# Joining the small TensorE steps of a pack attention that runs between the matmuls of an MLP

## The chip, the cores and the metric

The kernel runs on one core of a Trainium2 chip. The metric is the device time in microseconds (us) of one execution. The engines named here are TensorE (PE; PEld is its weight load), VectorE (DVE), ScalarE (ACT), GpSimd (POOL) and SyncE (SP), whose queue issues most DMAs.

## What is computed

A pack attention over 8 batches and 8 heads, with 576 rows and 64 columns per head and 32 packed rows, then two MLPs over its 4608 x 512 output. The reference, cut:

```python
def _attn_ref(q, k, v, p):
    scale = 1.0 / np.sqrt(q.shape[-1])
    def sm_attn(qq, kk, vv):
        s = scale * np.matmul(qq, kk.transpose(0, 1, 3, 2))
        s = s - np.max(s, axis=-1, keepdims=True)
        a = np.exp(s)
        a = a / (np.sum(a, axis=-1, keepdims=True) + 1e-09)
        return np.matmul(a, vv)
    p_packed = sm_attn(p, k, v)
    return sm_attn(q, p_packed, p_packed)

# x: 4608 x 512, w_in: 512 x 2048, w_out: 2048 x 512
h = x @ w_in;   x = (h * (1.0 / (1.0 + np.exp(-h)))) @ w_out          # first MLP
h = x @ w_in2;  out = (h * np.clip(h + 3.0, 0.0, 6.0) / 6.0) @ w_out2  # second MLP
```

## The kernel before

**Blocks.** The first MLP goes through nine blocks `j` of 512 token columns: one for the first 512 rows of each batch (blocks 0 to 7) and one for the 64 remaining rows, the tails, of all batches (block 8). In `block`, 16 slices `f` each have a hidden product (`hidden`, matmuls L874 to L876, one PSUM bank), a SiLU on ScalarE (L882), a split into a rounded part `gh` on ScalarE and a residue `gl` on VectorE (`split_g`, L889 and L890), and, two slices later, a projection (`project`, L897 to L899) into four accumulator banks. Each such matmul has 512 columns. Blocks 0 and 8 have twelve matmuls in a hidden product, blocks 1 to 7 six, since there the packed values have been multiplied into the first weights beforehand (`fuse_steps`, L657 to L659, the "fused" products). After block 8 the second MLP runs by itself.

**Attention between the matmuls.** A group `n` is four heads of a batch, two groups per batch, 16 in all. Groups 0 and 1 are done in an opening written out by hand. Groups 2 to 15 are done in small steps that are put between the big matmuls of blocks 0 to 6. Per group there are: the transposes of packed queries and of key and query tails (`step_kpq`), scores of packed queries against keys (`step_s`, L439) and against key tails (`step_st`, L449), a softmax (`exp1`, `post1`), transposes of its result (`step_t`, L471) and of its tail (`step_tt`, L479), the packed values (`step_pp`, L490 and L493), their transpose (`step_pt`, L513), scores of queries against packed values (called value scores here, `step_z`, L529, and `step_zt`, L538), a second softmax (`exp2`, `post2`), transposes on VectorE (`step_u`, `step_ut`) and the tail output (`step_xt`, L596). Keys and queries of groups from 4 on are transposed on VectorE (`step_tr`, L426). The products of scores and value scores use 64 columns of the array for each half of the heads, and each float32 product is two passes, so a step of this kind has four matmul records.

**PSUM.** Every small step takes a bank by `bank()`. Outside the opening this is the ring of four banks that the hidden products use as well. Four other banks are the accumulators.

**The order.** `WINDOWS` lists for each block which group `c` has its scores and which group `d` its value scores in a window; `b` and `a` are the `c` and `d` of the window before, whose softmaxes come in between. `window` turns that into steps with a cost, what they need and how long they wait behind it. A `Plan` counts ticks, one for each big matmul, and runs a step at a tick when its place in the block has come, its needs are met for so many ticks, and its bank is taken to be free. `hidden` offers a tick behind each half of a hidden product (in blocks 1 to 7), `block` one behind each quarter of a projection. What is left at a block's end is run there by `plan.finish`, with no big matmuls between.

**Loads.** `use` marks an operand as used; `load_next` then issues the loads of the values, queries and keys three entries further in the order of use, on SP's queue (L356, L366, L373). The same queue issues the weight tiles of the first MLP (`next_out`, L260, and `next_in`, L247).

Of the kernel before, what the change touches and what calls it, by code (L numbers as in the profile page):

```python
# [8 lines left out]
F32 = mybir.dt.float32  # L9
# [9 lines left out]
def tile_pack_attention_two_mlps(ctx: ExitStack, tc, q, k, v, p, w_in1, w_out1, w_in2, w_out2, out):  # L19
# [378 lines left out]
    def step_kpq(c, d):  # L398

        ps = bank()  # L400
        if c is not None:
            nc.tensor.transpose(ps[:, 0:P], pair(st.pop(("pbd", c)), 0), ident)
        for a, what, n in (1, "k", c), (2, "q", d):
# [3 lines left out]
            if n is not None:  # L407
                del nat[what, n]
        if c is not None:
# [12 lines left out]
    def step_tr(n, what, j):  # L422
        m = nat.pop((what, n, j))
        if n >= 4:
            t = half_kb(n, "T", 3)
# [5 lines left out]
        t = half_kb(n, "T", 3)  # L431
        copy(out=t, in_=ps)
        st[what, n, j] = t

    def step_s(n):
        kpq = st["kp", n]
        ps = bank()
        for j in range(2):
            mm(ps[j * 64:(j + 1) * 64, :], lhsT=kpq[:, j * 64:j * 64 + 64], rhs=st.pop(("k", n, j)), start=True, stop=True)  # L439
        d1 = d1s.pop(n) if n in d1s else at.tile([P, S], F32, tag="d1", name="d1")  # L440
        copy(out=d1[:, 0:T], in_=ps)
        st["d1", n] = d1

    def step_st(n):
        kpq, d1 = st.pop(("kp", n)), st["d1", n]
        ps = bank()
        for j in range(2):
            o = P + j * TAIL
            mm(ps[j * 64:(j + 1) * 64, 0:TAIL], lhsT=kpq[:, j * 64:j * 64 + 64], rhs=kpq[:, o:o + TAIL], start=True, stop=True)  # L449
        copy_short(out=d1[:, T:S], in_=ps[:, 0:TAIL])  # L450
        m = at.tile([P, 4], F32, tag="s1m", name="s1m", bufs=2)
        nc.vector.reduce_max(out=m[:, 0:1], in_=d1, axis=AX.X)
        nc.vector.tensor_scalar_mul(out=m[:, 1:2], in0=m[:, 0:1], scalar1=-SCALE)
        st["d1", n] = d1, m
# [11 lines left out]

    def step_t(n):
        d1, _ = st["d1", n]
        ps = bank()
        for i in range(NI):  # L470
            nc.tensor.transpose(ps[:, i * P:(i + 1) * P], d1[:, i * P:(i + 1) * P], ident)  # L471
        a = half_kb(n, "T", 3)
        copy(out=a, in_=ps)
        st["a1", n] = a

    def step_tt(n):
        d1, _ = st.pop(("d1", n))
        ps = bank()
        nc.tensor.transpose(ps[0:TAIL, 0:P], d1[:, T:S], ident)  # L479
        a = at.tile([TAIL, P], F32, tag="a1Tt", name="a1Tt")  # L480
        copy_short(out=a, in_=ps[0:TAIL, 0:P])
        st["a1t", n] = a
# [1390 lines left out]
```

## Time and profile before

| | |
|---|---|
| median of 3 runs | 1543.95 us (1542.73 to 1549.97) |
| the profiled execution | 1546.56 us, span 1544.7 us |
| TensorE matmuls in flight | 1505.0 us, 97% of the span |
| VectorE, ScalarE, GpSimd busy | 67%, 51%, 12% |
| mean granted TensorE clock | 0.994 of full speed |
| blocks 0 to 6 of the first MLP | about 38 to 686 us |
| blocks 7 and 8 | to about 846 us |

Times in the views are us from the first instruction unless marked ns. Matmuls are pipelined: a duration reaches from the start of one to the end of its drain, and the next begins before that, so costs on TensorE are read from start times. In a timeline row the brackets tell how long the engine was idle before the instruction and what ended it. L12 is line 12 of the kernel; `128*64 128x512` is a matmul over 128 rows and 64 columns of the array with 512 moving columns, and abank is a bank from `bank()`.

### The profile page before, as it was taken

How to read it: one execution, taken by the hardware profiler on the slowest of the kernel's cores; microseconds unless marked ns; L12 is line 12 of the kernel's file. 1: busy time of each engine (PE TensorE's matmuls, PEld its weight loads, DVE VectorE, ACT ScalarE, POOL GpSimd, SP SyncE). 2: the span in 40 equal slices, each digit the busy share in tenths (PEclk: the TensorE clock that was granted, in tenths of full speed). 3: DMA queues.
4: the chain of work that ended last, by engine and by line, in shares of the span. 5: the costliest groups of instructions: out<-in, count | busy, mean ns of one | idle time of the engine just before them, and what ended most of it. 6: DMA issues, size and time to landing. Idle time of an engine off the chain costs nothing.

```text
span 1544.7 us, 21698 instructions
## 1 busy us (share of the span) xinstructions
PE 1505.0 (97%) x7550; PEld 1224.5 (79%) x7550; DVE 1036.0 (67%) x1695; ACT 780.1 (51%) x1241; POOL 192.5 (12%) x177
## 2 busy tenths in 40 slices
PE   7999999999999999999999999999999999999998
PEld 4667766777777767778887888888888888999998
DVE  6667455755576556653452678877887778778777
ACT  6776546655565446654453334433443444444442
POOL 2433111111211111113241000000000000000000
PEclk9999999999999999999999999999999999999999
DMA  9999787987679777769697667677767776898887
GB/s 241 290 287 313 249 220 208 264 216 195 179 223 253 204 163 214 252 167 245 187 301 213 191 198 241 197 222 225 238 193 223 227 229 201 279 316 254 272 273 218
DMA packets 434508, 358.51 MB, mean 232 GB/s; under 512 B 191200, under 2 KB 325856, under 8 KB 434400
## 3 DMA queue, kind: packets, MB, share of 16 engines
q1 hardware_dynamic: 423632, 343.79, 75.8%
q10 hardware_dynamic: 10768, 13.34, 2.8%
q8 instruction: 61, 1.00, 0.3%
q14 instruction: 47, 0.39, 0.1%
HBM read 295.17 MB, written 61.87 MB: 231 GB/s over the span
## 4 chain that ended last, share of the span: by engine, by line
PE 84%; ACT 5%; DVE 4%; DMA 3%; SPq 2%; issue 2%; POOL 1%; ACTq 0%; DVEq 0%; POOLq 0%
PE b L1148 7%; PE b L1150 7%; PE b L1149 7%; PE b L1243 7%; PE acc L897 7%; PE b L1245 7%; PE b L1246 7%; PE acc L898 7%; PE acc L899 7%; PE hps L874 4%; PE hps L876 4%; PE hps L875 4%; PE abank L439 1%; PE abank L657 1%; PE abank L529 1%
## 5 line engine op out<-in xcount | busy, mean ns | idle before, releaser
L890 DVE TENSOR_TENSOR gl<-hps,gh 128x512 fp32r<-128x512 f32 x144 | 98.8, 686 | 165.9 <-ACT gh L889 165.5
L1245 PE MATMUL b<-ro,ws 128*128 128x512 f32 (+2 forms) x564 | 206.2, 366 | 0.0
L1246 PE MATMUL b<-ro,ws 128*128 128x512 f32 (+2 forms) x564 | 206.2, 366 | 0.0
L1148 PE MATMUL b<-xc,ws 128*128 128x512 f32 (+1 forms) x560 | 205.6, 367 | 0.0
L1150 PE MATMUL b<-xc,ws 128*128 128x512 f32 (+1 forms) x560 | 205.6, 367 | 0.0
L1149 PE MATMUL b<-xc,ws 128*128 128x512 f32 (+1 forms) x560 | 205.5, 367 | 0.0
L1191 DVE TENSOR_TENSOR ro<-g,ro 128x1024 fp32r<-128x1024 f32 (+1 forms) x140 | 161.4, 1157 | 42.1 <-ACT ro L1186 41.8
L1186 ACT CAST ro<-g 128x1024 fp32r<-128x1024 f32 (+1 forms) x140 | 132.1, 967 | 93.8 <-DVE g L1179 34.5
L882 ACT ACTIVATE hps<-hps 128x512 f32<-128x512 f32 x144 | 84.1, 584 | 113.9 <-PE hps L876 113.2
L1243 PE MATMUL b<-ro,ws 128*128 128x512 f32 (+2 forms) x564 | 139.0, 367 | 0.3
L897 PE MATMUL acc<-gh,wr 128*128 128x512 f32 x288 | 117.5, 408 | 3.2 <-ACT gh L889 3.2
L897 PE MATMUL acc<-gh,wo 128*128 128x512 f32 x288 | 116.8, 406 | 0.0
L1245 PEld LDWEIGHTS b<-ro,ws 128*128 128x128 f32 x564 | 105.9, 188 | 13.1
L1246 PEld LDWEIGHTS b<-ro,ws 128*128 128x128 f32 x564 | 105.9, 188 | 13.1
L1150 PEld LDWEIGHTS b<-xc,ws 128*128 128x128 f32 x560 | 105.1, 188 | 13.2
L1149 PEld LDWEIGHTS b<-xc,ws 128*128 128x128 f32 x560 | 105.1, 188 | 13.2
L1148 PEld LDWEIGHTS b<-xc,ws 128*128 128x128 f32 x560 | 105.1, 188 | 13.1
L1243 PEld LDWEIGHTS b<-ro,ws 128*128 128x128 f32 x564 | 102.9, 188 | 15.1 <-DVE ro L1191 2.2
L898 PE MATMUL acc<-gl,wr 128*128 128x512 f32 x288 | 113.8, 395 | 0.5 <-DVE gl L890 0.5
L899 PE MATMUL acc<-gh,wr 128*128 128x512 f32 x288 | 113.3, 393 | 0.0
L898 PE MATMUL acc<-gl,wo 128*128 128x512 f32 x288 | 112.6, 391 | 0.5 <-DVE gl L890 0.5
L899 PE MATMUL acc<-gh,wo 128*128 128x512 f32 x288 | 112.6, 391 | 0.0
(310 smaller groups left out, 2899.7 us busy)
## 6 DMA issues: line engine op xcount, KB each, us to landing
ws<-w2in SPq DMA_DIRECT2D x280, 256.0 KB, 3.2
ws<-w2out SPq DMA_DIRECT2D x280, 256.0 KB, 3.4
wi<-w1i SPq DMA_DIRECT2D x80, 512.0 KB, 5.5
wo<-w1o SPq DMA_DIRECT2D x64, 512.0 KB, 5.5
x1d<-x SPq DMA_DIRECT2D x18, 512.0 KB, 5.6
w1i<-win SPq DMA_DIRECT2D x16, 512.0 KB, 6.9
praw<-in_moe_w_in_dram SPq DMA_DIRECT2D x32, 256.0 KB, 5.5
praw<-in_moe_w_out_dram SPq DMA_DIRECT2D x32, 256.0 KB, 5.8
```

Source lines behind the costliest of these rows:

```text
L890: nc.vector.tensor_sub(out=gl, in0=g, in1=f32(gh))
L897: mm(acc[e], lhsT=w[:, 0, s], rhs=gh, start=first, stop=False)
L898: mm(acc[e], lhsT=w[:, 0, s], rhs=gl, start=False, stop=False)
L899: mm(acc[e], lhsT=w[:, 1, s], rhs=gh, start=False, stop=last)
L1148: mm(ps, lhsT=wh, rhs=xs[k][:, 0, c], start=first, stop=False, skip_group_check=True)
L1149: mm(ps, lhsT=wh, rhs=xs[k][:, 1, c], start=False, stop=False, skip_group_check=True)
L1150: mm(ps, lhsT=wl, rhs=xs[k][:, 0, c], start=False, stop=last, skip_group_check=True)
L1186: nc.scalar.copy(out=t[:, 0], in_=v)
L1191: nc.vector.tensor_sub(out=t[:, 1], in0=self.operand(s), in1=f32(t[:, 0]))
L1243: mm(to, lhsT=wh, rhs=x, start=False, stop=last, skip_group_check=True)
L1245: mm(to, lhsT=wh, rhs=x, start=first, stop=False, skip_group_check=True)
L1246: mm(to, lhsT=wl, rhs=x, start=False, stop=False, skip_group_check=True)
```

## The change

`step_kpq` now also does the transposes of `step_t` and `step_tt` for the group before, in two banks. `step_zs` replaces `step_z`, `step_zt`, `step_s` and `step_st`: value scores, scores, both tails, and, outside block 0, the transpose of packed values and the tail output of the groups before, in three banks; the engines that read them come behind all products. In block 1 the value scores of groups 4 and 5 move one window back. The planner lets one step take several banks and finish several keys, holds a fourth tile of transposed data (`T`, four buffers for three, in all functions that allocate it), and takes the loads of the next values when the joined step is issued. The packed values of groups 0 and 1 get tiles of their own in place of ones that weight tiles use later. `step_pt` and `step_xt` are cut in two, product and copy. The steps that these replace are taken out; the rest of the diff passes the new arguments on.

```diff
-    def step_kpq(c, d):
-
+    def step_kpq(c, d, b):
+
+        if b is not None:
+            d1, _ = st.pop(("d1", b))
+            rows = bank()
+            for i in range(NI):
+                nc.tensor.transpose(rows[:, i * P:(i + 1) * P], d1[:, i * P:(i + 1) * P], ident)
         ps = bank()
+        if b is not None:
+            nc.tensor.transpose(ps[0:TAIL, 3 * P:], d1[:, T:S], ident)
         if c is not None:
             nc.tensor.transpose(ps[:, 0:P], pair(st.pop(("pbd", c)), 0), ident)
...
+        if b is not None:
+            st["a1", b] = half_kb(b, "T", 4)
+            copy(out=st["a1", b], in_=rows)
+            st["a1t", b] = at.tile([TAIL, P], F32, tag="a1Tt", name="a1Tt")
+            copy_short(out=st["a1t", b], in_=ps[0:TAIL, 3 * P:])
         if c is not None:
             t = at.tile([P, 2 * P], F32, tag="kp", name="kp")
             copy(out=t, in_=ps[:, 0:2 * P])
...
     def value_pp(n, ps):
         r = st.pop(("r1", n))
         if n < QPB:
-            pf, on = half_kb(1, "ppf")[:, 0:HQ * D].rearrange("p (h d) -> p h d", h=HQ), mask
+            pf, on = at.tile([P, HQ, D], F32, tag="ppf0", name="ppf0", bufs=2), mask
         else:
             pf, on = at.tile([P, 2, D], F32, tag="ppf", name="ppf", bufs=3), twos
...
+    def step_pt(n, ps=None):
+        ps = bank() if ps is None else ps
+        nc.tensor.transpose(ps[:, 0:P], pair(st["pp", n], 0), ident)
+        st["ps", "pt", n] = ps
+
+    def step_ptc(n):
         t = at.tile([P, P], F32, tag="ppT", name="ppT", bufs=4)
-        copy_short(out=t, in_=ps[:, 0:P])
+        copy_short(out=t, in_=st.pop(("ps", "pt", n))[:, 0:P])
         st["ppT", n] = t
 
 
...
+    def step_zs(c, d, b, a):
+
+        if d is not None:
+            t, z = st["ppT", d], bank()
+            for j in range(2):
+                o = (1 - j if turned(d // QPB) else j) * 64
+                mm(z[o:o + 64, :], lhsT=t[:, j * 64:j * 64 + 64], rhs=st.pop(("q", d, j)), start=True, stop=True)
+        if c is not None:
+            kpq, ps = st.pop(("kp", c)), bank()
+            for j in range(2):
+                mm(ps[j * 64:(j + 1) * 64, :], lhsT=kpq[:, j * 64:j * 64 + 64], rhs=st.pop(("k", c, j)), start=True, stop=True)
+        rest = bank()
+        if d is not None:
+            qt = st.pop(("qt", d))
+            for j in range(2):
+                mm(rest[j * 64:(j + 1) * 64, TAIL:2 * TAIL], lhsT=t[:, j * 64:j * 64 + 64], rhs=qt[:, j * TAIL:(j + 1) * TAIL], start=True, stop=True)
+        if c is not None:
+            for j in range(2):
+                o = P + j * TAIL
+                mm(rest[j * 64:(j + 1) * 64, 0:TAIL], lhsT=kpq[:, j * 64:j * 64 + 64], rhs=kpq[:, o:o + TAIL], start=True, stop=True)
+        if b is not None:
+            step_pt(b, rest[:, P:2 * P])
+        if a is not None:
+            step_xt(a, rest[:, 2 * P:3 * P])
+        if d is not None:
+            nc.vector.transpose(out=d2s[d][:, 0:T], in_=z)
+        if c is not None:
+            d1 = d1s.pop(c) if c in d1s else at.tile([P, S], F32, tag="d1", name="d1")
+            copy(out=d1[:, 0:T], in_=ps)
+        if d is not None:
+            nc.vector.transpose(out=d2s[d][:, T:S], in_=rest[:, TAIL:2 * TAIL])
+            g = S // NP
+            m = at.tile([P, g, 1], F32, tag="s2m", name="s2m")
+            dv = d2s[d].rearrange("p (g s) -> p g s", s=NP)
+            nc.vector.reduce_max(out=m[:, :, 0], in_=dv, axis=AX.X)
+            nc.vector.tensor_tensor(out=dv, in0=dv, in1=m.to_broadcast([P, g, NP]), op=ALU.subtract)
+        if c is not None:
+            copy_short(out=d1[:, T:S], in_=rest[:, 0:TAIL])
+            m = at.tile([P, 4], F32, tag="s1m", name="s1m", bufs=2)
+            nc.vector.reduce_max(out=m[:, 0:1], in_=d1, axis=AX.X)
+            nc.vector.tensor_scalar_mul(out=m[:, 1:2], in0=m[:, 0:1], scalar1=-SCALE)
+            st["d1", c] = d1, m
+        if b is not None:
+            step_ptc(b)
+        if a is not None:
+            step_xtc(a)
...
-    WINDOWS = [[(2, None), (3, 2), (None, 3)], [(4, None), (5, 4), (6, 5), (7, None), (None, None)]]
+    WINDOWS = [[(2, None), (3, 2), (None, 3)], [(4, None), (5, None), (6, 4), (7, 5), (None, None)]]
     for j in range(2, B - 1):
...
+        def held(self, tile):
+            return tile and len(self.tiles) > 3 and self.tiles[-4] in self.open
+
+        def ready(self, key, need, tile, bank, count):
             if key[0] == "exps" and not self.calm:
                 return False
-            if bank and self.banks[0] > self.now:
+            if bank and self.banks[count == 3] > self.now:
                 return False
-            if tile and len(self.tiles) > 2 and self.tiles[-3] in self.open:
+            if self.held(tile):
                 return False
             return all(k not in self.open and self.done.get(k, -99) + wait * self.slow <= self.now for k, wait in need)
 
...
-            if bank:
+            for _ in range(count if bank else 0):
                 self.banks = [self.banks[1], max(self.now, self.late) + bank * self.slow]
...
-        add(c, "spread", 0, lambda: spread_p(c), ("kpq", b), bank=0)
-        add(c if c is not None else d, "kpq", 3 if c is not None else 1, kpq, ("spread", c), ("st", b), ("zt", a))
-        add(b, "t", 2, lambda: step_t(b), before[0], tile=("pp", b))
-        add(d, "q0", 0, lambda: step_tr(d, "q", 0), bank=0, tile=("z", d))
-        add(b, "tt", 1, lambda: step_tt(b), before[0])
-        add(d, "q1", 0, lambda: [step_tr(d, "q", 1), use("q", d)], ("q0", d), bank=0, tile=("z", d))
...
+        add(c, "spread", 0, lambda: spread_p(c), ("kpq", b), bank=0)
+        if b is not None:
+            add(b, "t", 2 + (2 if c is not None else 0), kpq, before[0], ("spread", c), tile=("pp", b), bank=7, count=2,
+                also=[("tt", b), ("kpq", either)])
+        else:
+            add(either, "kpq", 2, kpq, ("spread", c), bank=7)
+        add(d, "q0", 0, lambda: step_tr(d, "q", 0), (("k1", b), 0), (("t", b), 0), bank=0, tile=("z", d))
+        add(d, "q1", 0, lambda: [step_tr(d, "q", 1), use("q", d)], ("q0", d), bank=0, tile=("z", d))
+        add(b, "pp", 4, lambda: step_pp(b), ("t", b), ("tt", b))
         add(a, "u", 0, lambda: [step_u(a), step_ut(a)], before[1], bank=8)
-        add(b, "pp", 4, lambda: step_pp(b), ("t", b), ("tt", b))
-        add(a, "xt", 1, lambda: step_xt(a), ("u", a))
+        split_pt, split_xt = first or b == d, first
+        if split_pt:
+            add(b, "pt", 1, lambda: [alone(b, step_pt, step_ptc), use("v", b)], ("pp", b))
+        if split_xt:
+            add(a, "xt", 1, lambda: alone(a, step_xt, step_xtc), ("u", a))
+        add(c, "k0", 0, lambda: step_tr(c, "k", 0), (("pp", b), 0), (("q1", d), 0), bank=0, tile=("s", c))
+        add(c, "k1", 0, lambda: [step_tr(c, "k", 1), use("k", c)], ("k0", c), bank=0, tile=("s", c))
+        pt_, xt_ = None if split_pt else b, None if split_xt else a
+
+        def zs():
+            step_zs(c, d, pt_, xt_)
+            if pt_ is not None:
+                use("v", b)
+
+        keys = [("z", d), ("zt", d), ("s", c), ("st", c), ("pt", pt_), ("xt", xt_)]
+        lead = next((k for k in keys if k[1] is not None), None)
+        if lead:
+            add(lead[1], lead[0], (5 if d is not None else 0) + (5 if c is not None else 0) + 1, zs, ("pt", d), ("q0", d), ("q1", d), (("u", a), 0),
+                ("k1", c), ("kpq", either), ("tt", b), ("pp", pt_), ("u", xt_), bank=9, also=[k for k in keys if k != lead], count=3 if c is not None and d is not None else 2)
         add(a, "flush", 0, flush, ("xt", a), bank=0)
```

## Rows read from the trace of the kernel before

**Rows 1.** The page's engine table: busy us, share of the span, instructions.

```profile
PE 1505.0 (97%) x7550; PEld 1224.5 (79%) x7550; DVE 1036.0 (67%) x1695; ACT 780.1 (51%) x1241; POOL 192.5 (12%) x177
```

**Rows 2.** Timeline of TensorE, block 3: start us, us, engine, line, operation.

```profile
401.13 0.39 PE L876 MATMUL hps<-a2h,xh 128*128 128x512 f32 x1
401.45 1.08 PE L439 MATMUL abank<-T,kp 128*64 128x512 f32 x4
402.46 0.50 PE L897 MATMUL acc<-gh,wo 128*128 128x512 f32 x1
402.80 0.39 PE L898 MATMUL acc<-gl,wo 128*128 128x512 f32 x1
403.03 0.39 PE L899 MATMUL acc<-gh,wo 128*128 128x512 f32 x1
...
403.72 0.40 PE L899 MATMUL acc<-gh,wo 128*128 128x512 f32 x1
404.05 0.34 PE L449 MATMUL abank<-kp 128*64 128x64 f32 x4
404.31 0.50 PE L897 MATMUL acc<-gh,wo 128*128 128x512 f32 x1
```

**Rows 3.** Timeline of TensorE, the opening ahead of block 0.

```profile
24.93 1.08 PE L1500 MATMUL abank<-spare,ppT 128*64 128x512 f32 x4 [1.46 <-ACT spare L1384]
25.84 0.28 PE L1508 MATMUL abank<-spare,ppT 128*64 128x64 f32 x4
26.05 0.50 PE L1578 MATMUL unused<-win 128*128 128x512 f32 x1
```

**Rows 4.** Timeline of TensorE, block 3, attention transposes.

```profile
411.02 0.40 PE L876 MATMUL hps<-a2h,xl 128*128 128x512 f32 x1
411.26 0.60 PE L471 MATMUL abank<-ident,d 128*128 128x128 f32 x4
...
411.72 0.48 PE L897 MATMUL acc<-gh,wo 128*128 128x512 f32 x1
412.04 0.39 PE L898 MATMUL acc<-gl,wo 128*128 128x512 f32 x1
```

**Rows 5.** Timeline of TensorE, end of block 1.

```profile
255.47 0.65 PE L490 MATMUL abank<-nat,T 128*32 128x64 f32 x32 [0.57 <-ACT T L108]
...
257.19 0.30 PE L513 MATMUL abank<-ident,ppf 128*128 128x128 f32 x1 [0.82 <-DVE ppf L504]
258.20 0.50 PE L657 MATMUL abank<-wi,ph 128*128 128x512 f32 x1 [0.71 <-ACT ph L633]
...
262.54 0.50 PE L876 MATMUL hps<-a2h,fused 128*128 128x512 f32 x1 [0.82 <-DVE fused L665]
```

**Rows 6.** Timeline of TensorE, block 1, scores of group 6.

```profile
224.42 1.07 PE L439 MATMUL abank<-T,kp 128*64 128x512 f32 x2 [0.82 <-DVE T L426]
```

**Rows 7.** Timeline of ScalarE, block 0.

```profile
58.43 0.62 ACT L219 CAST wr<-cr 128x512 fp32r<-128x512 f32 x1 [2.11 <-PE abank L594]
```

**Rows 8.** VectorE's groups by line, 38 to 690 us: busy us, mean ns | idle.

```profile
L890 DVE TENSOR_TENSOR gl<-hps,gh 128x512 fp32r<-128x512 f32 x112 | 76.8, 685 | 99.6 <-ACT gh L889 99.1
...
L452 DVE TENSOR_REDUCE s1m<-d 128x1 f32<-128x576 f32 x14 | 10.5, 752 | 0.8
...
L111 DVE COPY xt<-abank 128x128 f32<-128x128 f32 x12 | 3.4, 285 | 2.7 <-PE abank L596 2.7
```

**Rows 9.** Timeline of SP's queue, block 2.

```profile
314.52 5.37 SPq L373 DMA_DIRECT2D nat<-in_q_dram  x8
...
326.71 7.80 SPq L373 DMA_DIRECT2D nat<-in_k_dram  x8
334.55 0.63 SPq L260 DMA_DIRECT2D wo<-w1o  x1
```

**Rows 10.** Timeline of TensorE, block 2, a projection's first matmul.

```profile
343.31 0.47 PE L897 MATMUL acc<-gh,wo 128*128 128x512 f32 x1
```

**Rows 11.** The page's DMA issues: queue, count, KB each, us to landing.

```profile
wo<-w1o SPq DMA_DIRECT2D x64, 512.0 KB, 5.5
```

More of the change, by code (lines that the diff above doesn't have):

```diff
@@ L430, in step_tr @@
         turn_rows(ps, m)
-        t = half_kb(n, "T", 3)
+        t = half_kb(n, "T", 4)
         copy(out=t, in_=ps)
         st[what, n, j] = t
[L435 to L454, printed above, removed]
     def exp1(n):
@@ L465, in post1 @@
         st["r1", n] = r
[L467 to L482, printed above, removed]
     def products_pp(n):
@@ L764, in run @@
             self.steps.remove(step)
-            _, key, cost, fn, _, tile, bank = step
+            _, key, cost, fn, _, tile, bank, count, also = step
             fn()
             self.now += cost
-            self.open.discard(key)
-            self.done[key] = self.now
+            for k in (key, *also):
+                self.open.discard(k)
+                self.done[k] = self.now
             if tile:
                 self.tiles.append(tile)
-            if bank:
+            for _ in range(count if bank else 0):
                 self.banks = [self.banks[1], max(self.now, self.late) + bank * self.slow]
@@ L782, in tick @@
             while i < len(self.steps) and self.steps[i][0] <= part:
[L783 removed]
+                if self.ready(self.steps[i][1], *self.steps[i][4:8]):
                     self.run(self.steps[i])
@@ L792, in finish @@
                 self.run(next(s for s in self.steps if not any(k in self.open for k, _ in s[4])
-                              and not (s[5] and len(self.tiles) > 2 and self.tiles[-3] in self.open)))
+                              and not self.held(s[5])))
     LATE = 24
@@ L797, in tile_pack_attention_two_mlps, with window, add @@
     plan = Plan()
-    def window(c, d, b, a):
+    def window(c, d, b, a, first):
         steps = []
         before = ("exps", b, a), ("ends", b, a)
-        def add(n, what, cost, fn, *need, tile=None, bank=5):
+        def add(n, what, cost, fn, *need, tile=None, bank=5, also=(), count=1):
             if n is not None:
-                steps.append(((what, n), cost, fn, need, tile, bank))
+                steps.append(((what, n), cost, fn, need, tile, bank, [k for k in also if k[1] is not None], count))
         def exps():
@@ L1760, in tile_pack_attention_two_mlps @@
         if 0 < j < B:
-            order.append((("xt", n), 1, lambda n=n: step_xt(n), (), None, 5))
-            order.append((("flush", n), 0, flush, (("xt", n),), None, 0))
+            order.append((("xt", n), 1, lambda n=n: [step_xt(n), step_xtc(n)], (), None, 5, (), 1))
+            order.append((("flush", n), 0, flush, (("xt", n),), None, 0, (), 1))
         for c, d in ws:
-            order += window(c, d, *last)
+            order += window(c, d, *last, j == 0)
             last = c, d
         total, sofar, at_pp = sum(s[1] for s in order), 0, 0
-        for key, cost, fn, need, tile, held in order:
+        for key, cost, fn, need, tile, held, also, count in order:
             sofar += cost
             place = sofar / total * (ATT.get(j, 0.83) if j < B - 1 else 0.2)
-            plan.add(key, place, cost, fn, [k if isinstance(k[0], tuple) else (k, (WAIT if j else FIRST).get(k[0], 0)) for k in need], tile, held)
-            if key[0] == "pt":
+            plan.add(key, place, cost, fn, [k if isinstance(k[0], tuple) else (k, (WAIT if j else FIRST).get(k[0], 0)) for k in need], tile, held, also, count)
+            if any(k[0] == "pt" for k in (key, *also)):
                 at_pp = place
```

68 lines of the change are left out of this document (20 added, 48 removed).

## The prediction

> **What bounds the kernel now.** I first read the page's engine table [rows 1]: TensorE has matmuls in flight for 97% of the span, so what TensorE does not have to do, or does with fewer interruptions, is time, and work of the other engines counts only where TensorE waits for it. Then I read TensorE's timeline in blocks 0 to 6, the part that the change touches, to see what one small attention step costs the stream of big matmuls around it [rows 2]. The reader is to compare start times: two ordinary matmuls of 512 columns start 0.23 us apart (402.80 and 403.03). The durations (0.39) overlap and are not to be added.
>
> A score step (two products, four passes, 64 columns of the array each) goes in at 401.13. The next big matmul starts at 402.46, 1.33 later where 0.23 is usual, and the one behind it another 0.34 later, again for 0.23. The step thus costs 1.10 + 0.11 = 1.21 us. A tail score step costs, from 403.72 to 404.31, 0.59 - 0.23 = 0.36, and with the same slow interval behind it 0.47, though it has an eighth of the columns. So much of a small step is fixed. [rows 3] show the only place where two such steps stand together: the value-score step starts at 24.93, its tail step follows 0.91 later, and the next big matmul 0.21 after that. Joined, the pair takes 1.12, with the entry seen in [rows 2] (401.45 - 401.13 - 0.23 = 0.09) and the slow interval behind (0.11) 1.32 us. Apart, 1.21 + 0.47 = 1.68. The join saves 0.36.
>
> Transposes over the whole array are another matter [rows 4]: five of them between 411.02 and 411.72 cost 0.70 - 0.23 = 0.47, plus 0.32 - 0.23 = 0.09 behind, 0.56 in all and 0.11 apiece. A lone one costs little more, so joining such transposes has nothing to win.
>
> **The change, part by part.**
> *Scores joined (the new step of scores, tails, packed transpose and tail output).* Groups 2 to 15 pass through these windows, 14 groups with four 64-column steps each, 56 runs in all. In the new list 11 windows have both a score group and a value-score group: their four runs become one, three joins each. Three windows have only scores and three only value scores: one join each. That is 33 + 6 = 39 joins. One join is worth at least the entry and the slow interval, 0.20, and at most the 0.36 of [rows 3]. I take 0.31, nearer to the row that shows a join: -12.1 us (bounds -7.8 and -14.0).
>
> *Transposes joined (attention rows, attention tail, packed queries, key and query tails).* By [rows 4] 0; if each lost 0.03 of a lone step, some 35 steps give at most -1. The tail transposes keep one run of their own shape. The packed transpose and the tail output in the score step likewise: 0.
>
> *The windows of block 1.* Value scores of groups 4 and 5 move one window back. Before, the last group's transpose, packed product and transpose come at the block's very end, with nothing between them, and TensorE waits 0.57 + 0.82 + 0.71 for their copies and 0.82 for the fused weights behind them [rows 5]: 2.9. In the new order each window is one chain of fewer links (softmax, transposes, packed product, one score step), and by the planner's costs (8, 14, 19, 19 and 7 for the five windows, 67 in all, spread over 0.8 of the block) the last transposes are due at (60 + 2) / 67 x 0.8 = 0.74 of the block, with a chain no longer held up by separate value scores. I expect that end to be covered by big matmuls: -2.9 (bounds 0 and -4).
>
> *Scores behind value scores.* One score run stood open for 0.82 while VectorE turned the second key tile [rows 6]. Value scores now run first and give such tiles 0.91 more: -1.0 (bounds 0 and -3).
>
> *Own tiles for packed values 0 and 1.* ScalarE stood for 2.11 us at a weight tile until a tail product had read the packed values that shared it [rows 7]. That goes; TensorE was not waiting for it, so 0 (bound -2).
>
> *One more transposed tile buffer (four for three).* It only relaxes a wait: 0.
>
> *What is added: bunched readers.* Behind the third bank VectorE now has, without a break, the tail transpose, a maximum and a subtraction over 576 columns, a copy, another maximum and three short operations. [rows 8] give 0.75 for a maximum, which I also take for the subtraction over the same columns, and 0.29 for the longest of the five short ones: 3 x 0.75 + 5 x 0.29 = 3.7 us. If the step is issued inside a hidden product, that product's residue (0.69 [rows 8]) queues behind this, and with it the release of its PSUM bank, which the next hidden product needs, because the step takes the three others. The joined run lasts about 0.09 + 4 passes' worth of [rows 3] (2 x 1.12) + three whole-array products of 0.11 = 2.7; readers begin near 2.9, VectorE is through at 6.6 and the residue at 7.3. TensorE wants the bank after 2.7 and twelve matmuls of 0.23, at 5.5, or 0.7 later if half a hidden product is still to come: a wait of 1.8 or 1.1. Where there is no packed transpose and tail output, about 0.5 less. I take 1.2 on average, in a third of the 11 windows (two of the six points at which a step can go in): +4.4 (bounds 0 and 11 x 1.8 = 19.8).
>
> Those times let readers of the third bank begin only after its last product, since the code issues all its products ahead of its first reader. The Trainium skill (PSUM — Partial Sum Buffer, section "PSUM bank collisions raise a hardware error") says that two engines must not be in one bank and the same 32 partitions at once, so a reader has to wait for products it does not use. Without that rule readers would begin about 0.33 earlier and the term would be 1.2 us smaller; no row here shows which holds.
>
> *What is moved: loads.* Values are declared used only when the joined step is issued, so in second windows the loads of the next values, queries and keys leave SP's queue in one bunch. Before, the eight key loads took SP 7.8 us, and a weight tile issued behind them at 334.55 [rows 9] was used at 343.31 [rows 10]. Now eight query loads (5.4) and four issues more (2.7 at the same rate) can stand ahead too. I take +2.0 (bounds 0 and 23, below).
>
> Sum: -12.1 - 2.9 - 1.0 + 4.4 + 2.0 = -9.6 us. The profiled execution took 1546.56, so 1537.0; the median of the runs shown is 2.6 lower, which gives 1534.4.
>
> **Rivals.** A measurement of this kernel can tell some 0.5%, 7.7 us, from no change: under 1536.2 is faster, over 1551.7 slower.
>
> *The bunch eats the gain (same).* If steps become ready mostly while a hidden product runs, two thirds of 11 windows wait about 1.45 us: +10.6 instead of +4.4, and 1540.6. For it: the readers' 3.7 us are real [rows 8]. Against: the consumer of a residue is a whole round behind, and only the bank ties it. The Trainium skill (TensorEngine Tiling (Array Packing), "PSUM Bottleneck") warns that packing the array speeds products but not the emptying of PSUM.
>
> *The change of shape is not what costs (same).* Were the fixed part paid by each small product, joins would save nothing: -2.9 - 1.0 + 6.4 = +2.5 and 1546.5. Against it stand [rows 3] and the cheap transposes of [rows 4].
>
> *The loads come late (slower).* One mechanism: SP's bunch of 20 issues ahead of a weight tile. The tile of [rows 9, 10] was issued 8.8 us before use; landing takes 5.5 in the median [rows 11], which leaves 3.3. With 8.1 us more ahead of it TensorE waits 4.8. In each of blocks 1 to 5 that is +24 in place of +2: 1534.4 + 22 = 1556. It decides from the point where more than 3.3 us of issues come ahead of the tile; against it, other tiles are issued well over 10 us ahead, and the query loads may be through earlier.
>
> **Chances.** My forecast 0.66, with its own range 1524 to 1539 (0.58 under 1536.2, 0.08 above). The bunch 0.14, the shape 0.06, the loads 0.14 (0.12 of it slower, 0.02 same). So faster 0.58, same 0.30, slower 0.12. The range is 1524 to 1544: the low end adds the better bounds of joins, block end and score waits to the sum and drops half of the bunch, the high end holds the bunch; left out are the late loads and some 0.05 below.
>
> **What would show it.** In TensorE's timeline after: one run per window with the value scores 0.9 long, scores behind them, and tail passes without big matmuls between; its cost near 2.5 us against 3.36 before. If the next big matmul after it starts as late as four separate steps, the first term is wrong. At the end of block 1 no waits for the copies. Waits of hidden products for a residue, with the tail transpose, maxima and subtraction ahead of it on VectorE, would show the bunch; waits of projections for a weight tile whose issue stands behind query and key loads, the loads. The prediction fails if waits in blocks 0 to 6 grow by more than the 12 us that the joins save.

## The result, and the profile after

| | before | after |
|---|---|---|
| median | 1543.93 us (6 runs) | 1528.42 us (1522.93 to 1530.43, 6 runs) |
| ratio, 95% interval | | 0.9885 [0.9861, 0.9909] |
| profiled execution | 1546.56 us, span 1544.7 | 1522.93 us, span 1521.0 |
| first MLP, from the first hidden product to the last projection | 809.2 us | 787.5 us |
| of that, waits of TensorE over 60 ns | 23.5 us | 23.8 us |
| of that, half of the time at a granted clock of 1.2 GHz | 5.8 us | 3.4 us |
| rest: products at 2.4 GHz | 779.9 us | 760.3 us |

The kernel is faster by 1.15% by the ratio and by 15.5 us, 1.0%, by the medians; 1528.4 lies 6 us under the forecast of 1534.4 and within its range. The last four lines are sums over all of TensorE's rows in that stage. I use them for every kernel below, because the rest hardly depends on which execution was profiled: in the changed kernel and in e2, e5, e6, e7 and e9, which have the same products, it is 759.1 to 760.5, while waits and clock differ. The profiled execution after is the shortest of its six, 5.5 us under their median, with a mean granted clock of 0.997 where four of the others have 0.992 to 0.995. The second MLP takes 698 us in both, the opening 37.2 and 35.7.

The page's engine table after, against [rows 1]:

```profile
PE 1481.4 (97%) x7550; PEld 1227.8 (81%) x7550; DVE 1038.6 (68%) x1695; ACT 779.7 (51%) x1241; POOL 193.8 (13%) x177
```

The same 7550 matmuls, in flight for 23.6 us less; the other engines do what they did. TensorE's timeline in block 0, a joined step with both scores, against [rows 2] and [rows 3]:

```profile
93.05 0.39 PE L924 MATMUL acc<-gh,wo 128*128 128x512 f32 x1
93.36 1.08 PE L506 MATMUL abank<-T,ppT 128*64 128x512 f32 x4
94.27 1.03 PE L510 MATMUL abank<-T,kp 128*64 128x512 f32 x4
95.13 0.28 PE L515 MATMUL abank<-qtT,ppT 128*64 128x64 f32 x4
95.25 0.29 PE L519 MATMUL abank<-kp 128*64 128x64 f32 x4
95.46 0.50 PE L922 MATMUL acc<-gh,wo 128*128 128x512 f32 x1
95.80 0.39 PE L923 MATMUL acc<-gl,wo 128*128 128x512 f32 x1
```

Start to start: 0.91 for the value scores, 0.86 for the scores, 0.12 and 0.21 for the tails. From 93.05 to 95.80, less two usual intervals of 0.23, the step costs 2.29; apart, the four cost 2 x 1.21 + 2 x 0.47 = 3.36. That is 1.07 for three joins, 0.36 each. Taken over all joined steps, with the interval not rounded, a join saves 0.354, and 39 of them 13.8 us.

A joined transpose step in block 3, against [rows 4]:

```profile
372.03 0.40 PE L901 MATMUL hps<-a2h,xh 128*128 128x512 f32 x1
372.26 0.60 PE L404 MATMUL abank<-ident,d 128*128 128x128 f32 x4
372.70 0.27 PE L407 MATMUL abank<-ident,d 128*64 128x128 f32 x1
372.81 0.27 PE L409 MATMUL abank<-ident,pbd 128*128 128x128 f32 x1
373.01 0.33 PE L413 MATMUL abank<-ident,kt 64*128 64x64 f32 x2
373.19 0.28 PE L413 MATMUL abank<-ident,qt 64*128 64x64 f32 x2
373.40 0.50 PE L922 MATMUL acc<-gh,wr 128*128 128x512 f32 x1
373.74 0.40 PE L923 MATMUL acc<-gl,wr 128*128 128x512 f32 x1
```

It costs 373.74 - 372.03 - 0.46 = 1.25, and the two separate steps of before cost 0.56 and 0.71: nothing is won. Note the jump of 0.20 from L409, over the whole array, to the first tail transpose over 64 rows (L413), where whole transposes follow each other at 0.11.

All waits over 0.7 us of TensorE in block 1 and at its end, where [rows 5] and [rows 6] were; the brackets give the wait and what ended it:

```profile
213.13 0.33 PE L413 MATMUL abank<-ident,qt 64*128 64x64 f32 x2 [0.75 <-DMA qt<-in_q_dram]
...
223.68 0.64 PE L510 MATMUL abank<-T,kp 128*64 128x512 f32 x1 [0.91 <-DVE T L438]
...
241.91 0.32 PE L467 MATMUL abank<-vt,a1Tt 64*32 64x64 f32 x8 [2.27 <-DVE a1Tt L111]
...
253.18 0.50 PE L901 MATMUL hps<-a2h,fused 128*128 128x512 f32 x1 [0.77 <-DVE fused L668]
...
257.16 0.47 PE L899 MATMUL hps<-a2h,fused 128*128 128x512 f32 x1 [1.17 <-DVE raw L668]
```

The wait for the second key tile is still there (0.91 for 0.82), the block's end still waits (2.27, 0.77 and 1.17), and a load is late, if only by 0.75: the query tail left SP's queue behind the values, 6 us ahead of its use.

```profile
205.87 1.10 SPq L366 DMA_DIRECT2D nat<-in_v_dram  x2
207.01 0.60 SPq L356 DMA_DIRECT2D qt<-in_q_dram  x1
```

For the key tile the brackets do not tell all. They count from the modelled end of the matmul before, so a shorter stop does not show. These rows of the kernel before, from TensorE's and VectorE's timelines of block 1, have no bracket, but the score steps last 1.70 and 2.10 where [rows 2] have 1.08; VectorE had the second key tile of the second one ready only at 195.62:

```profile
164.75 1.70 PE L439 MATMUL abank<-T,kp 128*64 128x512 f32 x4
...
194.66 2.10 PE L439 MATMUL abank<-T,kp 128*64 128x512 f32 x4
194.92 0.70 DVE L426 STREAM_TRANSPOSE T<-nat 128x512 f32<-128x512 f32 x1
```

By start times these two cost 0.61 and 1.02 more than 1.21, and the step of [rows 6] 1.90 more: 3.5 in all. After, only the step at 220.84 is held up, the one with the 0.91; it costs 4.56 where others of its kind cost 2.58, so 2.0.

The bunch of readers behind a joined step in block 2, in VectorE's timeline:

```profile
317.20 0.25 DVE L530 STREAM_TRANSPOSE d<-abank 128x64 f32<-128x64 f32 x1 [0.84 <-PE abank L596]
317.49 0.75 DVE L534 TENSOR_REDUCE s2m<-d 128x18 f32<-128x576 f32 x1
...
320.52 0.68 DVE L915 TENSOR_TENSOR gl<-hps,gh 128x512 fp32r<-128x512 f32 x1
...
321.84 0.29 DVE L330 TENSOR_TENSOR c<-c 128x128 f32<-128x128 f32 x1
```

It lasts from 317.20 to the residue at 320.52, 3.3 us for the 3.7 forecast, and the residue is there too. L530 reads columns that L515 wrote, but its wait ends with L596, the last product of that bank. The Trainium skill (PSUM — Partial Sum Buffer, section "PSUM bank collisions raise a hardware error") wants readers held off by bank, or by bank and 32 partitions, and not by address. This row shows the program doing so; no run shows what happens without it.

In this trace no hidden product of blocks 1 to 6 waits for a residue by over 0.4 us. But ScalarE and then TensorE wait for something else behind the bunch, first ScalarE:

```profile
322.16 0.73 ACT L333 CAST hi<-c 128x640 fp32r<-128x640 f32 x1 [3.65 <-DVE c L330]
...
325.31 0.78 ACT L449 ACTIVATE d<-d,s1m 128x576 f32<-128x576 f32 x1
```

and TensorE:

```profile
326.24 0.66 PE L404 MATMUL abank<-ident,d 128*128 128x128 f32 x4 [0.88 <-ACT d L449]
```

The conversion of the second MLP's weights (`c`, L327 to L330) stands on VectorE behind the bunch; ScalarE's cast of it (L333) holds up ScalarE's queue; the exponential behind it comes late, and the next transposes wait for that.

In block 0 three hidden products do wait for a residue: 1.14 at 43.35, 2.11 at 99.91 and 0.96 at 133.29. The longest, and VectorE's first reader of the joined step that went ahead of it, at 93.36:

```profile
99.91 0.50 PE L899 MATMUL hps<-xh,win 128*128 128x512 f32 x1 [2.11 <-DVE gl L915]
```

```profile
102.70 0.71 DVE L525 STREAM_TRANSPOSE d<-abank 128x512 f32<-128x512 f32 x1
```

So this wait is not one for the bunch, which VectorE begins 2.8 us later: block 0's weight conversion stands ahead of the residue there. At 133.29 it is the same, and 43.35 lies ahead of the first joined step.

Last, the clock. TensorE waited 2.15 us for an exponential up to 540.20. The view of stretches (time, busy us of PE, PEld, DVE, ACT and POOL with instructions, granted clock, DMA share, GB/s) shows what followed:

```profile
541.70:545.20 3.50, 3.50 (x9) 2.27 (x7) 2.14 (x6) 2.13 (x3) 0.00 (x0) 0.51 0.55 163
```

From 541.70 to 545.20 TensorE ran at 0.51, the 1.2 GHz level, behind the wait, and lost 1.7 us more; the stretch after it, to 555, has 1.00 again. The wait of 2.11 at 99.91 has such a stretch behind it too, at 101.4; the wait of 2.27 at 241.91 has none.

### The profile page after: what moved, and what is told of

It reads as the page before. It is cut to its first block, busy times and chain, and to the rows that moved or that the text cites. A ratio compares the mean times of both kernels' runs of the same rounds, so it can differ in the third digit from the quotient of the medians.

```text
span 1521.0 us, 21714 instructions
## 1 busy us (share of the span) xinstructions
PE 1481.4 (97%) x7550; PEld 1227.8 (81%) x7550; DVE 1038.6 (68%) x1695; ACT 779.7 (51%) x1241; POOL 193.8 (13%) x177
## 4 chain that ended last, share of the span: by engine, by line
PE 83%; DVE 4%; ACT 4%; DMA 3%; SPq 2%; issue 1%; POOL 1%; ACTq 0%; DVEq 0%; POOLq 0%
PE b L1174 8%; PE b L1175 8%; PE b L1173 8%; PE b L1268 8%; PE b L1271 7%; PE b L1270 7%; PE acc L922 7%; PE acc L923 7%; PE acc L924 7%; PE hps L899 4%; PE hps L901 4%; PE hps L900 4%; SPq L373 1%; DMA w1i<-win 1%; PE abank L660 1%
```

## The experiments

All are edits of the changed kernel, with 5 to 12 executions each. "Rest", "waits" and "clock" are the lines of the table above, for the profiled execution.

| | median us | ratio to before | rest | waits | clock |
|---|---|---|---|---|---|
| changed kernel | 1528.4 | 0.9885 [0.9861, 0.9909] | 760.3 | 23.8 | 3.4 |
| e1 scores apart | 1548.2 | 1.0042 [1.0028, 1.0056] | 776.6 | 28.4 | 7.2 |
| e2 transposes apart | 1532.4 | 0.9937 [0.9923, 0.9951] | 759.1 | 26.5 | 8.9 |
| e3 whole transposes behind | 1531.0 | 0.992 [0.990, 0.994] | 763.9 | 21.9 | 3.4 |
| e4 whole transposes between | 1538.4 | 0.9966 [0.9955, 0.9978] | 774.5 | 21.6 | 8.5 |
| e5 old windows | 1532.1 | 0.992 [0.9902, 0.9939] | 760.1 | 26.4 | 5.7 |
| e6 longer bunch | 1555.1 | 1.0063 [1.0045, 1.0081] | 759.5 | 42.8 | 18.8 |
| e7 values early | 1529.2 | 0.9899 [0.9881, 0.9918] | 760.5 | 27.0 | 3.9 |
| e8 stacked tails | 1527.0 | 0.9885 [0.9866, 0.9904] | 752.6 | 26.5 | 9.1 |
| e9 scores' readers first | 1529.9 | 0.9898 [0.9882, 0.9915] | 759.6 | 25.1 | 7.5 |
| e10 stacked tails, values early | 1533.2 | 0.9923 [0.991, 0.9936] | 752.8 | 30.7 | 13.0 |
| e11 the same, transposes later | 1554.5 | 1.0071 [1.0058, 1.0085] | 751.9 | 44.9 | 22.8 |
| e12 longer bunch, transposes later | 1570.5 | 1.0166 [1.015, 1.0181] | 757.4 | 53.8 | 22.2 |

**e1: the joined score step taken apart.** The four old steps in place of `step_zs`, the transpose of packed values and the tail output by themselves, the attention transposes still joined.

```diff
+        add(d, "z", 4, lambda: step_z(d), ("pt", d), ("q0", d), ("q1", d), (("u", a), 0), bank=9)
+        add(d, "zt", 1, lambda: step_zt(d), ("z", d), ("kpq", either))
+        add(c, "s", 4, lambda: step_s(c), ("k1", c), ("kpq", c), ("tt", b))
+        add(c, "st", 1, lambda: step_st(c), ("s", c))
```

> The changed kernel, with the joined score step taken apart again into value scores, their tails, scores, their tails, packed transpose and tail output, each a step of its own; the joined transposes, the new windows of block 1 and the tiles stay. If the array's change of shape is what costs (39 joins at 0.35 us by the changed kernel's timeline), the time rises by about 13.8 us over the changed kernel, to about 1542, and the single steps cost 1.21 and 0.47 again. If the gain came from the order and its waits, which stay mostly as they are, it stays within 5 us of 1528.

1548.2, slower than before. The rest grows by 16.3, and the single steps cost 1.21 and 0.47 again; 4.6 us of waits and 3.8 of clock come on top. By the medians that is 19.8 us over the changed kernel, more than the 15.5 that the change gains: this join carries the whole gain.

**e2: the transposes taken apart.**

```diff
-            step_kpq(c, d, b)
+            step_kpq(c, d)
...
+        add(b, "t", 2, lambda: step_t(b), before[0], tile=("pp", b))
+        add(b, "tt", 1, lambda: step_tt(b), before[0])
```

> The changed kernel, with the attention transposes, the attention tail and the transposes of packed queries and tails as three steps again; the joined score step stays. If only runs of another array shape cost, nothing is lost: 14 joins at 0.02 us, 0.3 us, so 1528 to 1529. If every separate step has a price of its own, or if the later packed-query step helps through the waits, it rises by 3 us or more.

1532.4: slower than the changed kernel, and the intervals do not overlap. The products cost nothing more (rest 759.1). In the profiles waits are 2.7 and the clock 5.5 dearer. With its own step, the query tail is wanted earlier and the load is not there:

```profile
218.27 0.47 PE L406 MATMUL abank<-ident,qt 64*128 64x64 f32 x2 [5.43 <-DMA qt<-in_q_dram]
```

Another 2.22 goes to a query tail at 193.51. In the changed kernel such waits come to 0.75.

**e3 and e4: whole-array transposes added to the joined step,** three in a two-sided step and one in a one-sided, in e3 behind the scores, in e4 one between each two of the four products.

```diff
+        def whole(n):
+            for _ in range(n):
+                nc.tensor.transpose(rest[:, 3 * P:], ident, ident)
```

> The changed kernel, with three added whole-array transposes (one in windows that have only scores or only value scores) behind the four runs of the joined score step; their output is not read. 39 of them at 0.11 us: 4.3 us over the changed kernel, about 1532, by every theory. It is the measure for the kernel that has the same transposes between the runs.

> The changed kernel, with the same 39 whole-array transposes put between the runs of the joined score step (value scores, transpose, scores, transpose, tails, transpose, tails), so that the array goes back to its whole shape after each run although the step stays joined. If the change of shape costs, this is 39 x 0.35 = 13.7 us slower than with the transposes behind, about 1546. If the price belongs to a separate step or to each small product, the two are equal.

e3 takes 1531.0, near the 1532 expected. e4 has the same instructions in another order. TensorE's timeline of e4, the step shown above for the changed kernel:

```profile
93.66 0.39 PE L936 MATMUL acc<-gh,wo 128*128 128x512 f32 x1
93.98 1.08 PE L513 MATMUL abank<-T,ppT 128*64 128x512 f32 x4
94.99 0.33 PE L507 MATMUL abank<-ident 128*128 128x128 f32 x1
95.25 1.08 PE L519 MATMUL abank<-T,kp 128*64 128x512 f32 x4
...
97.65 0.39 PE L935 MATMUL acc<-gl,wo 128*128 128x512 f32 x1
```

It costs 97.65 - 93.66 - 0.46 = 3.53; in e3 the same step costs 2.58. That is (3.53 - 2.58) / 3 = 0.32 for each place where a whole product parts 64-column ones. The rest differs by 10.6 us over 39 such places, the medians by 7.4 with intervals that do not overlap; I had expected 13.7. The direction decides between the theories: with equal products and equal steps the kernel with more changes between 64 columns and the whole array is slower.

**e5: block 1's windows as before.**

```diff
-[(4, None), (5, None), (6, 4), (7, 5), (None, None)]
+[(4, None), (5, 4), (6, 5), (7, None), (None, None)]
```

> The changed kernel with the windows of block 1 as they were: value scores of groups 4 and 5 one window earlier again. The number of joins stays (two windows with both, two with one). If the new windows had covered the block's end, as forecast (-2.9), undoing them gives +2.9: 1531.3 us, and TensorE's waits near the end of block 1 grow by about 3. If they gained nothing, which the changed kernel's trace suggests (waits of 2.27, 0.77 and 1.17 us still stand near the end of block 1), it stays within 2 us of 1528.4.

1532.1, 3.7 above the changed kernel; the intervals just overlap. That is the size of the first theory, but not its mechanism, since the waits at the block's end do not grow: 0.82, 0.71 and 1.56 where the changed kernel has 2.27, 0.77 and 1.17. The rest is the same, waits and clock are 2.6 and 2.3 higher: TensorE waits 2.25 for the second key tile at 235.25 and 1.51 for packed values at 208.14.

**e6: a longer bunch.**

```diff
-            nc.vector.reduce_max(out=m[:, :, 0], in_=dv, axis=AX.X)
+            for _ in range(6):
+                nc.vector.reduce_max(out=m[:, :, 0], in_=dv, axis=AX.X)
```

> The changed kernel with the first maximum of the joined step done six times in place of once, in the 14 steps that have value scores: 5 x 0.75 = 3.75 us more for VectorE in the bunch behind the step, 52 us in all, nothing else changed. If hidden products have slack outside block 0, as the changed kernel's trace suggests, only block 0's two steps can pay in full: up to +7.5, 1528 to 1536 us. If the bunch ties the hidden product's bank in a third of the windows, as forecast, five windows pay the whole 3.75: +19, about 1547 us. If in all of them, +52.

1555.1: all three theories miss. The price, +26.7, is higher than the forecast's mechanism gives, yet hidden products of blocks 1 to 6 wait for a residue by 0.29 at most, and those of block 0 hardly longer than in the changed kernel (1.10, 2.17 and 0.45). Of 19.0 us of added waits 10.2 are at the first transposes of the next window: 1.46, 2.96, 0.61, 4.81, 1.12, 2.32 and 1.11, all for an exponential, 14.4 in all where the changed kernel has 4.2. The longest, in VectorE's, ScalarE's and TensorE's timelines and in the view of stretches:

```profile
331.62 4.69 DVE L535 TENSOR_REDUCE s2m<-d 128x18 f32<-128x576 f32 x6
```

```profile
340.24 0.72 ACT L333 CAST hi<-c 128x640 fp32r<-128x640 f32 x1 [7.60 <-DVE c L330]
```

```profile
344.30 1.11 PE L404 MATMUL abank<-ident,d 128*128 128x128 f32 x4 [4.81 <-ACT d L449]
```

```profile
343.00:350.00 7.00, 5.70 (x16) 4.70 (x17) 3.16 (x8) 5.99 (x10) 0.00 (x0) 0.51 0.89 275
```

It is the chain seen at 326.24, 3.9 us longer: bunch, conversion, ScalarE's cast, exponential, transposes. The other waits are not all of this kind. For those of 2.96, 1.12 and 1.11 the exponential itself waits on ScalarE for its maximum (1.01, 1.73 and 1.73), which stands in the bunch; the 2.32 stands behind a load, as the 2.15 of the changed kernel does. The 8.8 of added waits elsewhere were not followed up. Behind the wait of 4.81 TensorE runs at 1.2 GHz up to 350, and over the stage the lower level costs 15.4 more, nearly as much as the waits (19.0).

**e7: values declared used with the packed product.**

```diff
-        add(b, "pp", 4, lambda: step_pp(b), ("t", b), ("tt", b))
+        add(b, "pp", 4, lambda: [step_pp(b), use("v", b)], ("t", b), ("tt", b))
```

> The changed kernel with values declared used right behind the packed product, a step before the joined one, so that their loads leave SP's queue earlier and not in one bunch with queries and keys. If the bunched loads cost the 2.0 us that the forecast has, 1526.4 us; if SP's queue has slack everywhere, as the changed kernel's trace suggests (no projection waits for a weight tile), 1528.4, within 2.

1529.2, no change clear of noise. The wait for the query tail is gone, but in block 0 a hidden product now waits 5.54 for a residue at 106.79, where it waited 2.11: ScalarE stands 4.66 there until the converted weights have been stored.

**e8: key and query tails stacked on 128 partitions.** For groups from 2 on.

```diff
-            for j in range(2 if n is not None else 0):
-                o = a * P + j * TAIL
-                nc.tensor.transpose(ps[:, o:o + TAIL], pair(nat[what, n], j), ident[0:TAIL, 0:TAIL])
             if n is not None:
+                nc.tensor.transpose(ps[:, a * P:(a + 1) * P], pair(nat[what, n], 0), ident)
```

> The changed kernel with the key tails, and the query tails, of a group loaded stacked on 128 partitions (two loads for one), so that one transpose over the whole array takes the place of two over 64 rows. If the change of the array's shape is what costs (about 0.31 us per excursion), the step with 4 tail transposes falls by 0.26 to 0.35 us, in 11 windows, and by about 0.2 in the 6 with one kind: -4 to -5 us, 1524 us. If columns streamed are what costs, two passes of 128 take as long as four of 64: no change, or some tenths more for 28 loads more on SP's queue, 1528.4 to 1530.

The step without the attention's own transposes, at the end of block 1:

```profile
264.22 0.39 PE L666 MATMUL abank<-wi,pl 128*128 128x512 f32 x1
264.45 0.27 PE L415 MATMUL abank<-ident,pbd 128*128 128x128 f32 x1
264.56 0.27 PE L418 MATMUL abank<-ident,kt 128*128 128x128 f32 x1
264.66 0.27 PE L418 MATMUL abank<-ident,qt 128*128 128x128 f32 x1
264.69 0.48 PE L926 MATMUL acc<-gh,wr 128*128 128x512 f32 x1
265.01 0.39 PE L927 MATMUL acc<-gl,wr 128*128 128x512 f32 x1
```

It costs 265.01 - 264.22 - 0.46 = 0.33, where the changed kernel's costs 0.71; the rest falls by 7.7. So 64 rows are as dear as 64 columns (0.37 here, 0.35 for a join), and the step does win. But the median is 1527.0, within noise of the changed kernel's. In the two profiles waits rise by 2.7 and the clock takes 5.7, some of it perhaps only because the changed kernel's profile is its shortest. The query tail, now two loads, holds TensorE up:

```profile
217.98 0.30 PE L418 MATMUL abank<-ident,qt 128*128 128x128 f32 x1 [2.66 <-DMA qt<-in_q_dram]
```

**e9: the scores' readers first.** The block of `copy_short` and maximum for the scores ahead of that for the value scores' tail, maximum and subtraction; nothing else.

> The changed kernel with two blocks of readers behind the joined step exchanged: the scores' tail copy and maximum come ahead of the value scores' tail transpose, maximum and subtraction, so that the first softmax has its maximum 1.7 us earlier. Nothing is added or removed. In the changed kernel's trace the next window's transposes wait for that softmax in places (0.59, 0.59, 0.88 and 2.15 us). If the softmax is late because its own maximum stands behind the value scores', these waits shrink: 1523 to 1526 us. If ScalarE is late for other reasons (it waits 3.65 us for a weight conversion that stands behind the whole bunch on VectorE, and 4.5 us for a load at another place), nothing changes: within 2 us of 1528.4.

1529.9, no change. The waits for exponentials stay (1.44, 0.81, 0.87 and 1.27 us). At the bunch's normal length the softmax is not late for its own maximum; ScalarE's queue is. What holds that queue up differs: in the changed kernel the cast that waits 3.65 for a conversion, ahead of 326.24, and a wait of 4.52 for a load, ahead of 540.20.

**e10 and e11: e8 and e7 together; and with the planner's wait behind the exponentials raised** (in block 0 from 14 to 17).

```diff
-            "exps": 18, "ends": 18,
+            "exps": 22, "ends": 18,
```

> Stacked tails and early use of values together. With stacked tails alone (1527.0) the tail transposes cost 0.37 us less in each of 17 steps, 6 us by TensorE's start times, but one step waited 2.66 us for the load of the query tail, with a stretch at half clock behind it, and the waits for softmax grew; with early values alone that wait was gone. Together, if the load is what took the gain back: 1527.0 - 2.7 - 1.7 = 1522.6 us. If time only moves on to the next wait, 1526 to 1529.

> As the kernel with stacked tails and early values, with the transposes of the softmax's rows put off by four ticks (three in block 0) of the planner. If the waits for the softmax (1.46, 1.43, 0.88 and 1.25 us with stacked tails) vanish, with one or two of the half-clock stretches behind them: 5 to 8 us less than without the delay, about 1516 to 1518 us. If the windows, longer by four ticks each, push their last steps into the blocks' ends, the waits there take it back: 1523 or more.

e10 misses both of its forecasts with 1533.2: the wait for the query tail is gone, and 5.93 for a residue at 106.64 in block 0 and 2.01 for a weight tile at 255.46 have come. e11 takes 1554.5, which its second theory leaves open, but the time does not go where that has it. The waits for exponentials are gone, as expected, yet it is not the block's end that takes it back: in ten windows the packed product now waits 0.9 to 3.2 us for the copy of the tail (`a1Tt`).

**e12: e6 with the transposes later** (`exps` 24, in block 0 20).

> The kernel with the maximum done six times (1555.1), with the transposes of the softmax's rows put off by six ticks (1.4 to 2.0 us). If the long bunch costs because ScalarE's exponentials, queued behind conversion work that stands behind the bunch, reach these transposes late (waits of 1.46, 2.96, 0.61, 4.81, 1.12, 2.32 and 1.11 us, 14.4 in all, and half-clock stretches behind them), most of these waits go: 14.4 falls to about 4, and with fewer half-clock stretches the time to 1535 to 1545 us. If the hidden products' bank pays, as the forecast has the bunch, no change: 1553 to 1557.

1570.5. The waits for exponentials fall from 14.4 to 4.6, as the theory has it, and the time still rises by 15. In ten windows the packed product now waits 0.9 to 3.0 us for the copy of the tail, 22.8 in all. TensorE and VectorE in block 2:

```profile
306.28 0.27 PE L407 MATMUL abank<-ident,d 128*64 128x128 f32 x1
...
313.43 0.44 PE L467 MATMUL abank<-vt,a1Tt 64*32 64x64 f32 x8 [2.79 <-DVE a1Tt L111]
```

```profile
310.75 0.15 DVE L454 TENSOR_SCALAR r<-s1m 128x1 f32<-128x1 f32 x1
...
313.09 0.28 DVE L111 COPY a1Tt<-abank 64x128 f32<-64x128 f32 x1
```

And VectorE in the changed kernel, where the tail's transpose starts at 326.73:

```profile
326.21 0.15 DVE L454 TENSOR_SCALAR r<-s1m 128x1 f32<-128x1 f32 x1 [1.49 <-ACT d L449]
...
328.77 0.28 DVE L111 COPY a1Tt<-abank 64x128 f32<-64x128 f32 x1
```

In both, six operations of the softmaxes' second half, from L454 on, stand on VectorE ahead of the copy. In the changed kernel they start 0.5 us ahead of the tail's transpose and the copy follows it by 2.0; here they start 4.5 behind it, and the copy follows by 6.8. The wait of 2.27 at 241.91 in the changed kernel is one of this kind: there they start 3.1 behind. The planner's number that e11 and e12 raise holds this second half back as well as the transposes, so neither run shows what later transposes alone would do.

## Why the prediction was right or wrong

**The joins** carried it, and the mechanism was right: the fixed part of a small product is the change of the array's shape, paid once for each run of such products. The rival that had it otherwise fell with e4 and e8. The term's size was too low: 0.31 taken, 0.354 measured, 13.8 us for 12.1, near the bound from [rows 3]. I had drawn the value away from the one row that showed a join, without a row against it.

**The joined transposes:** 0 was right for the products, as the 1.25 against 0.56 + 0.71 and e2's rest show. That undoing them costs 4 us (e2), by waits and the clock, was not seen: a step that is issued later, with another, also wants its load later.

**The windows of block 1.** The step "I expect that end to be covered" failed: 2.27 + 0.77 + 1.17 = 4.2 us of waits stand where 2.9 were. With the joined step the old order is slower still by some 3.7 us (e5), but the intervals just overlap, and the waits that it adds lie elsewhere in the block.

**Scores behind value scores.** The forecast read 0.82 in [rows 6], where by start times late second key tiles cost block 1 3.5 us. The term of -1.0 has the right size, 3.5 to 2.0, but its mechanism is not shown. Groups 4 and 5, whose scores are held up no longer, have no value scores ahead of them in the new windows; group 6 has them and runs freely; group 7 has them and is late by 0.91 all the same.

**The bunch** was mis-sized and put at the wrong place. Its length was right (3.3 for 3.7), but blocks 1 to 6 show no wait of a hidden product for a residue that would matter, so neither the term's 4.4 nor the rival's 10.6 came about by the bank. The three residue waits of block 0 (1.14, 2.11 and 0.96, against 1.21 and 0.64 of small steps before) do not stand behind a bunch. The bunch does cost, by a path that the forecast lacks: conversion work queued behind it on VectorE, ScalarE's cast of that, the exponential, the next window's transposes. With the bunch as it is, 0.88 at 326.24 is the one wait that the rows shown lead back to it. With 3.75 us more in each of 14 steps the kernel loses 26.7 (e6), of which this chain is 3.9 and the rest other waits and the clock; no run takes the conversion out from behind the bunch.

**The loads.** No projection waits for a weight tile, so the rival fell. The mechanism was right with another victim: the query tail, behind the values on SP's queue, costs 0.75 here, 2.44 in e9, which leaves the loads as they are, and 2.66 in e8, where it is two loads. +2.0 lies between these, and undoing it gives nothing: in e7 the wait for the query tail is gone, and one of 5.54 in block 0 has come. The bound of 23 and the rival's +24 should be the same number.

In sum, by the first table's lines, for the two profiles (-23.7 where -9.6 was forecast): the rest fell by 19.6 for 12.1. Of that 13.8 are the joins, and 2.0 that a wait costs some 0.2 beyond its idle time, by start times, and the stage has 23 waits for 32. Another 1.6 is what the late second key tiles cost beyond their brackets (2.7 before, 1.1 after); 2.2 I could not place. Waits rose by 0.3 for 2.5. The clock gave 2.4, the opening and the second MLP 2.0, none of it forecast; among the six executions of the changed kernel alone the mean granted clock goes from 0.992 to 0.998. The medians leave most of such chance out: 15.5 us, 5.9 better than the sum. That the sum came so near is in part luck, since -2.9 for the block's end and +4.4 for the bunch both failed, with opposite signs. The range is wider than its working too: by the bounds named, 1.9, 1.1 and 2.0, and half of the bunch, 2.2, its low end would be 1527 and not 1524; 1528.4 lies inside either.

## What to carry to other kernels

Count how often TensorE goes from the whole array to 64 columns or 64 rows and back, not the small products: read from start times, each excursion cost about a third of a us here, and putting a few small products behind one another, or stacking two halves on 128 partitions, removes it. Such a gain need not arrive where a load or a queue is just in time: in e8 the products gave 7.7 us, and in the two profiles waits and clock took it back. A bracket of idle time is not the whole price of a wait: compare the length of a step with that of its like. When a bunch of readers is moved onto one engine, follow what is queued behind it on that engine through to the next engine's queue; here one wait came out two engines further on.

## What was not expected of the hardware

A wait cost more than its length. Behind waits of 2.15 and 4.81 us TensorE ran at 1.2 GHz for 3.5 and some 7 us. In e6 the added waits were 19.0 us, and the lower clock took 15.4 more. The Trainium skill (TensorE: Matmul & The Clock Gate, section "What's actually happening") has idleness bring the lower level, and these rows agree in that both stretches stand behind a wait; the wait of 2.27 at 241.91 without such a stretch shows that length alone does not decide.

With it goes the spread of equal kernels: the six runs of the changed kernel, with spans from 1521.0 to 1528.6 us, have mean granted clocks of 0.997 and 0.998 for the two shortest and 0.992 for the longest. A difference below some 4 us between two kernels here, half the width of the ratio's interval, can be nothing but which waits met the clock, and one profile against another is worse than the medians: 23.7 us against 15.5.
